# Token tiles' products: a float32 transpose by TensorE into the h banks and a split there, in place of a DMA transpose of the two split parts

## The chip, the cores and the metric

The kernel runs on one core of a Trainium2 chip, in one launch. The metric is the device time of that launch in microseconds; the median of three runs of the kernel before is 2922.66 us (2917.66 to 2924.61).

## What is computed

Three layers, one after the other, on 8 sequences of 3072 tokens with 256 channels: a filter in the frequency domain, a SoLU block with a layer norm, and a routed layer with eight experts.

```python
X = np.fft.rfft(x, axis=1)
y = np.fft.irfft(X * (filt_r + 1j * filt_i)[None], n=x.shape[1], axis=1)   # attn
x = y.reshape(B * S, D)
h = x @ w_in                                    # 256 -> 1024
e = np.exp(h - h.max(-1, keepdims=True))
sm = e / (e.sum(-1, keepdims=True) + 1e-09)
solu = h * sm
mu = solu.mean(-1, keepdims=True); var = ((solu - mu) ** 2).mean(-1, keepdims=True)
x = (((solu - mu) / np.sqrt(var + 1e-06)) * g_ln) @ w_out       # 1024 -> 256
xn = x / (np.linalg.norm(x, axis=-1, keepdims=True) + 1e-06)
logits = xn @ en.T / tau                        # en: unit expert embeddings
expert_idx = logits.argmax(1); probs = softmax(logits)
out[mask_e] = probs[.., e] * (np.maximum(x[mask_e] @ w1[e], 0) @ w2[e])
```

## The kernel before

The 24576 tokens go through as 192 tiles of 128 tokens, 48 for each of four pairs of sequences. Stage A is the FFT of a pair (`fft`, first stage at L487, second at L601 with the result z, the filter at L562 and L563, third at L635); the inverse's last stage is `inv4` (L672), which gives two tiles at once. Stage B (`stage_b`) takes the tiles one after the other through w_in and w_out and routes them. Stage C (`stage_c`) runs the experts over blocks of the tokens routed to them.

The order is the order of the code: `tc.manual_schedule()` leaves every engine's instructions as they are issued, and each engine works through its own list in order. Stage B is a loop over i with several tiles in flight:

- `begin(i + 1)` issues the 12 float32r matmuls of h (L688) into one of two PSUM tiles h of two banks each; `top(i + 1)` lets VectorE take the negative maximum nm (L828);
- for tile i ScalarE writes es = Exp(h + nm) (L840), VectorE multiplies h with es into es (L841, the "product"), ScalarE squares the product into h (L877), which gives the sum of squares for the factor cc (L886);
- for tile i - 1 ScalarE copies the product times cc to float16 (hl, L853), VectorE writes the rest to the other half of hl (L854), and SP transposes both, 128 x 2048 float16, by a DMA into T (L856);
- for tile j = i - LAG (LAG = 3) TensorE multiplies T with w_out in 24 float16 matmuls into o (L868); `half`, an iteration later, splits o into two float16 parts and SP stores them (rows, L894 to L899).

Beside the tiles of pair p the function `aux`, called twice per iteration, runs units of the FFT of pair p + 1: 24 units of its first stage, 8 with loads only, 64 of the second and third stage in groups of four (two z units, two third-stage units; the filter of the group before stands at the third). Beside the last pair it splits the experts' weights (`w_split`, L427 and L433). The FFT's loads and stores, the tiles' loads and stores and the transposes all go out on SP's queue. `early` makes the first tables of stage C beside the last tiles, one step per iteration.

Of the kernel before, what the change touches and what calls it, by code (L numbers as in the profile page):

```python
# [23 lines left out]
FF = 1024  # L24
# [9 lines left out]
LAG = 3  # L34
# [5 lines left out]
MAGIC = 0x5F3759DF  # L40

# [71 lines left out]
class Tags:  # L113
    """A pool with a number of buffers for each tag."""
# [16 lines left out]
class Tag:  # L131
    """One tag of a pool."""
# [6 lines left out]
class Turns:  # L139
    """A pool whose buffers are taken in turn."""  # L140
# [10 lines left out]
class Build:  # L151
# [72 lines left out]
    def scale(self, ps, sp, m, sc, isc):  # L224
        """[128, n] -> sc = 2^k with 4 <= max(m) * sc < 8, isc = 1 / sc, on all partitions."""
# [24 lines left out]
    def load_wide(self, out, src):  # L250
        """Loads 512 columns of float32, or of float64 (given as its bits), which it rounds to float32."""
# [25 lines left out]
    def prep_b(self, sp, ps):  # L277
        """MoE weights: w_in as two float32r parts; g * w_out, centred, with its product with the
        experts' embeddings, as two float16 parts."""
# [7 lines left out]
        def unit():  # L287
            """Unit embeddings, transposed."""
# [91 lines left out]
    def w_max(self, sp, ps):  # L380
        """Scales of the experts' weights: powers of two from their largest magnitudes."""
# [17 lines left out]
    def w_split(self, sp):  # L399
        """The experts' weights, resident, as two float16 parts."""  # L400
# [37 lines left out]
    def rsqrt(self, v, w, y, x, tmp, shape):  # L438
        """y = x^-1/2 by Newton's steps from the bit-level start; tmp: twice x's columns."""
# [10 lines left out]
    # ---------------------------------------------------------------- stage A  # L450
# [21 lines left out]
    def stage1(self, p, part, ap, ps, bufA):  # L472
        """The transform over n1, with the twiddle factors, of a part of the columns."""
# [19 lines left out]
    def catch_up(self):  # L493
        """Work that was put off until the engines have time for it."""
# [4 lines left out]
    def fft(self, p, ap, ps, hp):  # L499
        """Stages 1 to 3 for the pair of batches p, as a stream of units; the first pair in two parts  # L500
        of the columns, so that their stages overlap."""
# [18 lines left out]
        def first(j):  # L520
            """The unit's first k1, in the order 0 to 31, 63 to 32."""
            return j % NK // 2 * KC + j % 2 * (N1 // 2)
# [125 lines left out]
    def inv4(self, xp, ps):  # L648
        """Stage 4: yields, for two tiles at once, x transposed as float32r parts."""
# [29 lines left out]
    # ---------------------------------------------------------------- stage B  # L679
# [20 lines left out]
    def b_final(self, t, p, n2, gw, ps, snap):  # L700
        """Routing of a group's tokens: their factors and their places in the experts' lists."""
        nc = self.nc
        v, w = nc.vector, nc.gpsimd
        st, cc, raw = t["st"], t["cc"], t["raw"]
        Se, Ss, Sq = st[:, 0, :], st[:, 1, :], st[:, 2, :]
# [8 lines left out]
        # x = r * (row of products); V = (variance + 1e-6) * (sum of exponentials)^2  # L714
        rc = row("grc", 2)
        v.reciprocal(rc, cc)
        V = row("gV", 2)
        u = row("gu")
        w.tensor_scalar(V[:, 0, :], Se, 1e-9, None, op0=ALU.add)
        w.tensor_tensor(V[:, 0, :], V[:, 0, :], V[:, 0, :], op=ALU.mult)  # L720
# [19 lines left out]
        w.tensor_tensor(r, y[:, 0, :], rc[:, 0, :], op=ALU.mult)  # L740
        w.tensor_scalar(r, r, self.isc_o, None, op0=ALU.mult)
# [9 lines left out]
        w.tensor_tensor(r, r, rc[:, 1, :], op=ALU.mult)  # L751
# [51 lines left out]
    def stage_b(self, xp, bps, gp, ps, hp, op, aux, early):  # L803
        """aux(p, n2): runs the units that belong beside tile n2 of the pair p."""
# [19 lines left out]
        def top(i):  # L824
            L = live[i]
            L["pool"] = bps[0] if i < n - N2 else bps[1]
            L["nm"] = L["pool"].tile([128, 1], F32, name="nm", tag="nm")
            nc.vector.tensor_reduce(L["nm"], L["h"], axis=AX.X, op=ALU.max, negate=True)  # L828

        begin(0)  # L830
        top(0)
        for i in range(n + LAG):
            j = i - LAG
            now = 0 <= i < n
            if now:
                if i % G == 0:
                    groups[i // G] = self.b_group(gp)
# [3 lines left out]
                nc.vector.scalar_tensor_tensor(L["s"], L["h"], 1.0, L["s"], op0=ALU.mult, op1=ALU.mult, accum_out=col(i, "st", 1))  # L841
# [3 lines left out]
            if 0 <= i - 1 < n:  # L845
                M, cc = live[i - 1], col(i - 1, "cc", 0)
                P = M["pool"]
                if "hl" not in P.kept:
                    P.kept["hl"] = P.tile([128, 3 if P is bps[1] else 4, FF], F16, name="hl", tag="hl")
                r = 2 * ((i - 1) % 2)  # L850
                l = 1 if P is bps[1] else r + 1
                hl = P.kept["hl"]
                nc.scalar.activation(hl[:, r, :], M["s"], AF.Copy, scale=cc)  # L853
                nc.vector.scalar_tensor_tensor(hl[:, l, :], M["s"], cc, hl[:, r, :], op0=ALU.mult, op1=ALU.subtract)  # L854
                T = P.tile([128, 16, 128], F16, name="T", tag="T")
                nc.sync.dma_start_transpose(out=T, in_=hl[:, min(l, r):min(l, r) + 2, :].rearrange("p a b -> p (a b)"))  # L856
                M["T"] = (T, 8 if l < r else 0)
# [394 lines left out]
```

## Time and profile before

| | |
|---|---|
| median of three runs | 2922.66 us |
| profiled execution, span of its instructions | 2966.3 us |
| TensorE matmul / weight load | busy 2667.8 us (90%) / 2153.6 us (73%) |
| VectorE, ScalarE, GpSimd | busy 1920.5, 1447.2, 1445.9 us |
| stage A of the first pair alone | to about 215 us |
| stage B | about 215 to 1862 us |
| stage C | about 1862 us to the end |

The profile is one execution; for it only the span is known, and the timed runs are shorter than the span by 43.6 us, 1.5%. A busy TensorE is not one at its peak: a matmul's record has a length that overlaps with the next one's, so the pace is read from the distance between starts. Plain float32 matmuls are recorded as two.

### The profile page before, as it was taken

The page shows a single profiled execution, that of the slowest core. Times are in us where ns is not written, and L with a number is a line of the kernel's source. Part 1 is how long each engine was busy: PE and PEld are TensorE (multiplying, and loading weights), DVE is VectorE, ACT ScalarE, POOL GpSimd, SP SyncE. Part 2 cuts the span into 40 slices and gives each one's busy share as a digit, 9 for nine tenths or more (in the row PEclk, how much of TensorE's full clock was granted, in tenths as well). Part 3 has the DMA queues.
Part 4 walks back from the last instruction along what each step waited for, and adds up shares of the span by engine and source line. Part 5 has one row for each costly group of instructions (what it writes and reads, how often), then busy time and mean ns, then how long its engine had stood idle before and what let it go on. Part 6 is the DMA issues. An engine that isn't in the chain of part 4 may idle for free.

```text
span 2966.3 us, 52286 instructions
## 1 busy us (share of the span) xinstructions
PE 2667.8 (90%) x19262; PEld 2153.6 (73%) x19262; DVE 1920.5 (65%) x3013; ACT 1447.2 (49%) x2746; POOL 1445.9 (49%) x2237
## 2 busy tenths in 40 slices
PE   5788898989888988889998888899999999999997
PEld 4446666767666666656786677778888888888876
DVE  2755787856788855887878887445444444444454
ACT  3345666656556655556677776223333333333322
POOL 1420476623656523655647774654444444444432
PEclk8889998999889999989999999999999999999999
DMA  9869999899899999987878886222322222233222
GB/s 272 197 164 244 215 221 197 191 240 240 183 188 194 193 235 224 190 185 168 172 162 192 184 187 123 73 67 74 77 76 76 76 77 76 75 78 76 74 53 48
DMA packets 729551, 447.47 MB, mean 151 GB/s; under 512 B 535595, under 2 KB 656053, under 8 KB 726992
## 3 DMA queue, kind: packets, MB, share of 16 engines
q1 hardware_dynamic: 701920, 386.12, 60.4%
q0 software_dynamic: 27088, 57.48, 6.4%
q8 instruction: 152, 2.49, 0.4%
q14 instruction: 103, 0.84, 0.1%
q10 hardware_dynamic: 288, 0.55, 0.1%
HBM read 195.93 MB, written 103.35 MB: 101 GB/s over the span
## 4 chain that ended last, share of the span: by engine, by line
PE 32%; issue 22%; DMA 17%; POOL 16%; DVE 10%; ACT 2%; SPq 1%; POOLq 0%; another core or an unknown queue 0%; DVEq 0%; ACTq 0%
PE o L868 12%; DMA T<-hl 11%; PE h L688 9%; POOL crow L1039 6%; POOL out_dram L162 5%; POOL scr L161 3%; PE a L635 2%; PE a L487 2%; DVE hl L854 2%; PE a L672 2%; PE o L1106 1%; DMA mt<-in_m_dram 1%; DVE zw L562 1%; DVE nm L828 1%; PE a L601 1%
## 5 line engine op out<-in xcount | busy, mean ns | idle before, releaser
L868 PE MATMUL o<-wo_h,T 128*128 128x264 f16 x3072 | 602.2, 292 | 119.3 <-DMA T<-hl 67.4
L868 PEld LDWEIGHTS <-T 128*128 128x128 f16 x4608 | 469.0, 104 | 244.3 <-DMA T<-hl 82.8
L1106 PE MATMUL o<-cw,chh 128*128 128x256 f16 x3184 | 534.8, 274 | 10.3 <-ACT chh L1097 9.3
L1094 PEld LDWEIGHTS <-cw 128*128 128x128 f16 x5280 | 477.7, 98 | 60.1 <-issue 9.2
L162 POOL DMA_INDIRECT out_dram<-cot,ids x199 | 206.0, 1035 | 503.8 <-ACT cot L1109 492.2
L868 PE MATMUL o<-wo_l,T 128*128 128x264 f16 x1536 | 449.3, 293 | 0.0
L1106 PE MATMUL o<-cw,chl 128*128 128x256 f16 x1592 | 435.9, 274 | 10.9 <-DVE chl L1098 10.2
L1098 DVE SCALAR_TENSOR_TENSOR chl<-h,chh 128x512 f16<-128x512 f32 x199 | 136.1, 684 | 410.3 <-ACT chh L1097 392.4
L1106 PEld LDWEIGHTS <-chh 128*128 128x128 f16 x3184 | 309.9, 98 | 51.8 <-ACT chh L1097 16.0
L841 DVE SCALAR_TENSOR_TENSOR es<-h,es 128x1024 f32<-128x1024 f32 x192 | 234.9, 1223 | 171.5 <-ACT es L840 162.1
L688 PE MATMUL h<-win_h,xh 128*128 128x512 f32 x768 | 319.4, 416 | 1.3 <-ACT xh L675 0.7
L840 ACT ACTIVATE es<-h,nm 128x1024 f32<-128x1024 f32 x192 | 214.1, 1115 | 206.8 <-DVE gcc L886 194.8
L688 PE MATMUL h<-win_h,xl 128*128 128x512 f32 x768 | 302.4, 394 | 0.0
L1094 PE MATMUL a<-cxT,cw 128*128 128x256 f16 (+1 forms) x2640 | 296.4, 264 | 5.0 <-issue 5.0
L688 PE MATMUL h<-win_l,xh 128*128 128x512 f32 x768 | 300.3, 391 | 0.0
L1094 PE MATMUL h<-cxT,cw 128*128 128x256 f16 (+1 forms) x2640 | 295.4, 263 | 3.9 <-DVE cw L1067 3.9
L1109 ACT ACTIVATE cot<-o,fac 128x256 f32<-128x256 f32 x199 | 94.5, 475 | 419.0 <-PE o L1106 416.8
L1067 DVE COPY cw<-wexp 128x4096 f16 x220 | 279.6, 1279 | 22.3 <-issue 6.0
L854 DVE SCALAR_TENSOR_TENSOR hl<-es,gcc,hl 128x1024 f16<-128x1024 f32 x192 | 262.9, 1369 | 27.0 <-DMA T<-hl 18.1
L828 DVE TENSOR_REDUCE nm<-h 128x1 f32<-128x1024 f32 x192 | 233.5, 1216 | 65.4 <-PE h L688 64.8
L162 POOL DMA_INDIRECT lst<-gdi,gix x192 | 244.6, 1274 | 38.0 <-issue 26.8
L1039 POOL DMA_INDIRECT crow<-xs,ids x199 | 198.3, 997 | 72.2 <-issue 66.0
(239 smaller groups left out, 4594.0 us busy)
## 6 DMA issues: line engine op xcount, KB each, us to landing
wst<-in_w_dram SPq DMA_DIRECT2D x128, 256.0 KB
in<-in_x_dram SPq DMA_DIRECT2D x48, 512.0 KB
bufA<-out SPq DMA_DIRECT2D x96, 256.0 KB
in<-bufA SPq DMA_DIRECT2D x64, 384.0 KB
bufC<-out SPq DMA_DIRECT2D x128, 192.0 KB
c<-bufC SPq DMA_DIRECT2D x96, 256.0 KB
xs<-rows SPq DMA_DIRECT2D x96, 256.0 KB
ft<-in_filt_dram SPq DMA_DIRECT2D x24, 960.0 KB
```

The source lines that it names most:

```text
L162: ins = self.nc.gpsimd.indirect_dma_start(in_offset=None, **kw).ins
L688: nc.tensor.matmul(h[:, nb, :], l[:, i, db, :], r[:, db, sl], start=k == 0, stop=k == 5)
L828: nc.vector.tensor_reduce(L["nm"], L["h"], axis=AX.X, op=ALU.max, negate=True)
L840: nc.scalar.activation(L["s"], L["h"], AF.Exp, bias=L["nm"], accum_out=col(i, "st", 0))
L841: nc.vector.scalar_tensor_tensor(L["s"], L["h"], 1.0, L["s"], op0=ALU.mult, op1=ALU.mult, accum_out=col(i, "st", 1))
L854: nc.vector.scalar_tensor_tensor(hl[:, l, :], M["s"], cc, hl[:, r, :], op0=ALU.mult, op1=ALU.subtract)
L868: nc.tensor.matmul(o[:, :D + E], T[:, l, :], r[:, f, :], start=q == 0, stop=q == 23)
L1039: nc.gpsimd.indirect_dma_start(out=rows[:, h, :], out_offset=None, in_=self.xs, in_offset=bass.IndirectOffsetOnAxis(ap=tab["ids"][:, h, k: ...
L1067: nc.vector.tensor_copy(w.rearrange("p (o k) -> p o k", o=1), self.wexp[:, bass.ds(e, 1), part * 4096:(part + 1) * 4096])
L1094: nc.tensor.matmul(t[:, i, :], w1[:, l, db, f * 128:(f + 1) * 128], xT[:, r + db, :n], start=q == 0, stop=q == 5)
L1098: nc.vector.scalar_tensor_tensor(hl[:, sl, :n], t, 0.0, hh[:, sl, :n], op0=ALU.max, op1=ALU.subtract)
L1106: nc.tensor.matmul(o[:, :D], l[:, f, h * 128:(h + 1) * 128], w2[:, r, f, :], start=q == 0, stop=q == 23)
```

## The change

Per tile, `turn(i)` issues eight float32 transposes of the product es by TensorE into the tile's own h, whose values are no longer needed, 128 columns each. ScalarE then copies h times 16384 to the first half of T in float16, and VectorE writes the rest to the second half. hl and the DMA transpose are gone. So that h is not written by the square any more, the square goes to a bfloat16 buffer jk. The factor cc must be known before the product: it comes from nm with two column operations in `top`, and the product is taken with it; `b_final` follows suit. LAG is 2, `aux`'s first call stands ahead of `begin`, `early` starts two iterations later, and some start-up buffers have other names. The compiled program has 1536 more matmuls and as many more weight loads, eight of each for a tile.

```diff
-LAG = 3
+LAG = 2
+SS = 16384.0
...
-        rc = row("grc", 2)
-        v.reciprocal(rc, cc)
+        rc = row("grc")
+        v.reciprocal(rc, cc[:, 1, :])
...
         w.tensor_scalar(V[:, 0, :], Se, 1e-9, None, op0=ALU.add)
+        w.tensor_tensor(V[:, 0, :], V[:, 0, :], c1, op=ALU.mult)
...
-        w.tensor_tensor(r, y[:, 0, :], rc[:, 0, :], op=ALU.mult)
-        w.tensor_scalar(r, r, self.isc_o, None, op0=ALU.mult)
+        w.tensor_scalar(r, y[:, 0, :], self.isc_o, 1.0 / SS, op0=ALU.mult, op1=ALU.mult)
...
         def top(i):
+            if i % G == 0:
+                groups[i // G] = self.b_group(gp)
...
             nc.vector.tensor_reduce(L["nm"], L["h"], axis=AX.X, op=ALU.max, negate=True)
+            cc = col(i, "cc", 0)
+            nc.vector.tensor_scalar(cc, L["nm"], L["nm"], 1.0, op0=ALU.mult, op1=ALU.max)
+            nc.vector.tensor_scalar(cc.bitcast(I32), cc.bitcast(I32), -0.5, float(MAGIC), op0=ALU.mult, op1=ALU.add)
+
+        def turn(i):
+            M = live[i]
+            h = M["h"]
+            for f in range(8):
+                nc.tensor.transpose(h[:, f * 128:(f + 1) * 128], M["s"][:, f * 128:(f + 1) * 128], self.ident)
+            T = M["T"] = M["pool"].tile([128, 16, 128], F16, name="T", tag="T")
+            hi, lo = (T[:, k:k + 8, :].rearrange("p a b -> p (a b)") for k in (0, 8))
+            nc.scalar.activation(hi, h, AF.Copy, scale=SS)
+            nc.vector.scalar_tensor_tensor(lo, h, SS, hi, op0=ALU.mult, op1=ALU.subtract)
...
+            if 0 <= i - 1 < n:
+                turn(i - 1)
             if now:
...
-                nc.vector.scalar_tensor_tensor(L["s"], L["h"], 1.0, L["s"], op0=ALU.mult, op1=ALU.mult, accum_out=col(i, "st", 1))
+                nc.vector.scalar_tensor_tensor(L["s"], L["h"], col(i, "cc", 0), L["s"], op0=ALU.mult, op1=ALU.mult, accum_out=col(i, "st", 1))
...
-                nc.scalar.activation(hl[:, r, :], M["s"], AF.Copy, scale=cc)
-                nc.vector.scalar_tensor_tensor(hl[:, l, :], M["s"], cc, hl[:, r, :], op0=ALU.mult, op1=ALU.subtract)
-                T = P.tile([128, 16, 128], F16, name="T", tag="T")
-                nc.sync.dma_start_transpose(out=T, in_=hl[:, min(l, r):min(l, r) + 2, :].rearrange("p a b -> p (a b)"))
...
             if now:
+                aux(*divmod(i, N2), 0)
                 if i + 1 < n:
                     begin(i + 1)
-                aux(*divmod(i, N2), 0)
-                if i + 1 < n:
                     top(i + 1)
-                sq = col(i, "st", 2)
-                nc.scalar.activation(L["h"], L["s"], AF.Square, accum_out=sq)
+                jk = L["pool"].tile([128, FF], BF16, name="jk", tag="jk")
+                nc.scalar.activation(jk, L["s"], AF.Square, accum_out=col(i, "st", 2))
...
-                cc = col(i, "cc", 0)
-                nc.vector.tensor_scalar(cc.bitcast(I32), sq.bitcast(I32), -0.5, float(MAGIC + (14 << 23)), op0=ALU.mult, op1=ALU.add)
...
-            if i >= n - N2 + SPLIT:
+            if i >= n - N2 + SPLIT + 2:
                 next(early, 0)
```

Three places show how the engines' lists change. Line numbers of the kernel after are higher by a few.

VectorE before, in an iteration with the filter (zw, y); es is the product, hl the rest of the split, nm the maximum of the next tile:

```order
L841 SCALAR_TENSOR_TENSOR es,gst<-h,es 128x1024
L854 SCALAR_TENSOR_TENSOR hl<-es,gcc,hl 128x1024
L895 SCALAR_TENSOR_TENSOR rows<-o,gcc,rows 128x256
L562 SCALAR_TENSOR_TENSOR zw<-zw,cst,ft 96x1024
L563 TENSOR_TENSOR y<-y,zw 96x1024
L393 TENSOR_REDUCE wm_a<-wst 128x1
L828 TENSOR_REDUCE nm<-h 128x1
L886 TENSOR_SCALAR gcc<-gst 128x1
L889 COPY graw<-o 128x8
L890 TENSOR_SCALAR gcc<-gn_7528 128x1
```

VectorE after, in such an iteration and the first operation of the next; T written from h is the rest of the split:

```order
L847 SCALAR_TENSOR_TENSOR T<-h,T 128x1024
L860 SCALAR_TENSOR_TENSOR es,gst<-h,gcc,es 128x1024
L898 SCALAR_TENSOR_TENSOR rows<-o,gcc,rows 128x256
L563 SCALAR_TENSOR_TENSOR zw<-zw,cst,ft 96x1024
L564 TENSOR_TENSOR y<-y,zw 96x1024
L833 TENSOR_REDUCE nm<-h 128x1
L835 TENSOR_SCALAR gcc<-nm 128x1
L836 TENSOR_SCALAR gcc<-gcc 128x1
L892 COPY graw<-o 128x8
L893 TENSOR_SCALAR gcc<-gn_8186 128x1
L718 RECIPROCAL grc<-gcc 128x8
L847 SCALAR_TENSOR_TENSOR T<-h,T 128x1024
```

The rest of the split has moved from behind the product to the head of the iteration, ahead of it, and reads h.

TensorE before, from the end of h to the o of the next iteration, beside the FFT's third stage:

```order
L688 MATMUL h<-win_h,xh 128x512
L688 MATMUL h<-win_l,xh 128x512
L688 MATMUL h<-win_h,xl 128x512
L635 MATMUL a<-y,cst_95 96x512 x2
L672 MATMUL a<-mt_11363,c_11361 128x128 x4
L868 LDWEIGHTS T
L868 MATMUL o<-wo_h,T 128x264
```

TensorE after, the same stretch:

```order
L689 MATMUL h<-win_h,xh 128x512
L689 MATMUL h<-win_l,xh 128x512
L689 MATMUL h<-win_h,xl 128x512
L636 MATMUL a<-y,cst_95 96x512
L843 MATMUL h<-cst,es 128x128 x8
L673 MATMUL a<-mt_12442,c_12440 128x128 x4
L874 LDWEIGHTS T
L874 MATMUL o<-wo_h,T 128x264
```

The eight transposes stand between an iteration's last FFT unit and stage 4 or o; one of the two FFT units has gone ahead of h.

SP before, in the FFT's first stage (bufA is its result, wst a piece of the experts' weights, c and mt stage 4's input):

```order
L856 DMA_TRANSPOSE T<-hl 128x16x128
L899 DMA xs<-rows 128x512
L491 DMA bufA<-out 64x4x256 x2
L389 DMA wst<-in_w_dram 128x512
L659 DMA c_10284<-bufC 128x512
L661 DMA mt_10286<-in_m_dram 128x256
L856 DMA_TRANSPOSE T<-hl 128x16x128
```

SP after, at the end of that stage:

```order
L902 DMA xs<-rows 128x512
L492 DMA bufA<-out 64x4x256 x2
L531 DMA ft<-in_filt_dram 96x2560
L390 DMA wst<-in_w_dram 128x512
L537 DMA in<-bufA 96x1024 x2
L660 DMA c_11432<-bufC 128x512
```

Nothing stands between the loads and stores any more.

## Rows read from the trace of the kernel before

**Rows 1.** Busy time of each engine by stretch; then granted clock, DMA share, GB/s.

```profile
215.00:1512.00 1297.00, 1144.61 (x6602) 868.85 (x6602) 973.31 (x1601) 791.31 (x1540) 635.01 (x1075) 0.94 0.95 203
1512.00:1862.00 350.00, 303.74 (x2036) 248.20 (x2034) 286.56 (x596) 244.98 (x485) 225.51 (x440) 0.97 0.77 170
```

**Rows 2.** Waits of TensorE, 215 to 1512 us: total, times, longest.

```profile
PE o L868 <- DMA T<-hl: 67.4, 40, 5.8
PE a L601 <- DVE xl L676: 27.2, 16, 2.7
```

**Rows 3.** The stretches again, h matmuls (L688) alone: length, busy (xcount), then loads.

```profile
595.00:697.00 102.00, 32.94 (x132) 23.97 (x132) 0.97 1.07 244
697.00:736.00 39.00, 15.00 (x60) 10.90 (x60) 0.96 1.09 228
736.00:1006.00 270.00, 84.50 (x336) 61.26 (x336) 0.91 0.93 189
...
1512.00:1600.00 88.00, 39.04 (x156) 28.33 (x156) 1.00 0.78 177
1600.00:1841.00 241.00, 102.01 (x408) 74.09 (x408) 0.98 0.77 172
```

**Rows 4.** TensorE in order of time, two tiles: start us, length us, instruction.

```profile
514.45 0.27 PE L868 MATMUL o<-wo_h,T 128*128 128x264 f16 x1
...
517.06 0.48 PE L688 MATMUL h<-win_h,xh 128*128 128x512 f32 x1
...
519.90 0.40 PE L601 MATMUL a<-hi,d2h 96*96 96x512 f32 x1
...
521.46 1.16 PE L672 MATMUL a<-mt,c 128*128 128x128 f32 x8
522.45 0.28 PE L868 MATMUL o<-wo_h,T 128*128 128x264 f16 x1
...
527.92 1.88 PE L635 MATMUL a<-y,cst 96*96 96x512 f32 x4
529.63 0.28 PE L868 MATMUL o<-wo_h,T 128*128 128x264 f16 x1
```

**Rows 5.** SP's DMA transposes in the view of line L856: ns min/median/max.

```profile
L856 SPq DMA_TRANSPOSE T<-hl x192: 1317/3585/8397, 223.1 to 1854.5; - x192
```

**Rows 6.** Costliest groups of the page: busy us, mean ns | idle before.

```profile
L841 DVE SCALAR_TENSOR_TENSOR es<-h,es 128x1024 f32<-128x1024 f32 x192 | 234.9, 1223 | 171.5 <-ACT es L840 162.1
L840 ACT ACTIVATE es<-h,nm 128x1024 f32<-128x1024 f32 x192 | 214.1, 1115 | 206.8 <-DVE gcc L886 194.8
...
L854 DVE SCALAR_TENSOR_TENSOR hl<-es,gcc,hl 128x1024 f16<-128x1024 f32 x192 | 262.9, 1369 | 27.0 <-DMA T<-hl 18.1
```

**Rows 7.** TensorE's weight loads in order of time, at 63 and at 521 us.

```profile
63.05 0.97 PEld L330 LDWEIGHTS o<-penT,pwT 128*128 128x128 f32 x8
...
521.45 0.97 PEld L672 LDWEIGHTS a<-mt,c 128*128 128x128 f32 x8 [0.45 <-ACT z L602]
```

**Rows 8.** VectorE and TensorE in order of time around one filter.

```profile
1288.95 0.48 DVE L895 SCALAR_TENSOR_TENSOR rows<-o,gcc,rows 128x256 f16<-128x256 f32 x1
...
1289.35 3.09 DVE L562 SCALAR_TENSOR_TENSOR zw<-zw,cst,ft 96x1024 f32<-96x1024 f32 x1
...
1292.54 3.20 DVE L563 TENSOR_TENSOR y<-y,zw 96x1024 f32<-96x1024 f32 x1
...
1295.66 1.21 DVE L828 TENSOR_REDUCE nm<-h 128x1 f32<-128x1024 f32 x1
...
1300.10 0.48 PE L601 MATMUL a<-hi,d2h 96*96 96x512 f32 x1 [2.11 <-DVE xl L676]
```

**Rows 9.** The filter's first product in the view of its line: ns min/median/max.

```profile
L562 DVE SCALAR_TENSOR_TENSOR zw<-zw,cst,ft x48: 1265/3016/3205, 348.7 to 1465.8; 96x1024 f32<-96x1024 f32 x45, 96x768 f32<-96x768 f32 x3
```

**Rows 10.** TensorE in order of time: last h matmul, first expert matmul.

```profile
1838.93 0.39 PE L688 MATMUL h<-win_h,xl 128*128 128x512 f32 x1
...
1865.97 1.44 PE L1094 MATMUL h<-cxT,cw 128*128 128x256 f16 x6 [3.93 <-DVE cw L1067]
```

More of the change, by code (lines that the diff above doesn't have):

```diff
@@ L704, in b_final @@
         st, cc, raw = t["st"], t["cc"], t["raw"]
+        c1 = cc[:, 0, :]
         Se, Ss, Sq = st[:, 0, :], st[:, 1, :], st[:, 2, :]
@@ L750, in b_final @@
         w.tensor_tensor(d, raw, bc(rn), op=ALU.mult)
-        w.tensor_tensor(r, r, rc[:, 1, :], op=ALU.mult)
+        w.tensor_tensor(r, r, rc, op=ALU.mult)
         yield
@@ L834, in stage_b @@
             now = 0 <= i < n
+            if 0 <= i - 1 < n:
+                turn(i - 1)
             if now:
-                if i % G == 0:
-                    groups[i // G] = self.b_group(gp)
                 L = live[i]
@@ L844, in stage_b @@
                 xs.append(next(src, None))
[L845 to L852, printed above, removed]
-                nc.scalar.activation(hl[:, r, :], M["s"], AF.Copy, scale=cc)
-                nc.vector.scalar_tensor_tensor(hl[:, l, :], M["s"], cc, hl[:, r, :], op0=ALU.mult, op1=ALU.subtract)
-                T = P.tile([128, 16, 128], F16, name="T", tag="T")
-                nc.sync.dma_start_transpose(out=T, in_=hl[:, min(l, r):min(l, r) + 2, :].rearrange("p a b -> p (a b)"))
-                M["T"] = (T, 8 if l < r else 0)
             if half:
@@ L862, in stage_b @@
             if 0 <= j < n:
-                T, k = live.pop(j)["T"]
+                T = live.pop(j)["T"]
                 o = op.tile([128, 512], F32, name="o", tag="o")
@@ L866, in stage_b @@
                 for f in range(8):
-                    for l, r in ((k + f, self.wo_h), (k + f, self.wo_l), (8 - k + f, self.wo_h)):
+                    for l, r in ((f, self.wo_h), (f, self.wo_l), (8 + f, self.wo_h)):
                         nc.tensor.matmul(o[:, :D + E], T[:, l, :], r[:, f, :], start=q == 0, stop=q == 23)
@@ L973, in table @@
             in_offset=bass.IndirectOffsetOnAxis(ap=ri[:K].bitcast(U32), axis=0)).ins
+        assert len(self.scattered["lst"]) >= (self.np_run * N2 // G - (3 if start is None else 0)) * G
         for name in self.scattered["lst"]:
@@ L1134, in run @@
             bps = [None, None]
-            bps[0] = right.enter_context(Tags(tc, "bx", {"nm": 2, "es": 2, "hl": 1, "T": 3}, side="right"))
+            bps[0] = right.enter_context(Tags(tc, "bx", {"nm": 2, "es": 2, "jk": 1, "T": 3}, side="right"))
             ap = right.enter_context(tc.tile_pool(name="ap", bufs=2, side="right"))
@@ L1144, in run @@
                     prep = self.prep_b(pp, Tag(op, "o"))
-                    spare = bps[0].tile([128, 16, 128], F32, name="hl", tag="hl")
-                    self.m1 = [spare[:, 4 * k:4 * k + 4, :] for k in range(4)]
+                    spare = pp.tile([128, 12, 128], F32, name="m1s")
+                    self.m1 = [spare[:, 4 * k:4 * k + 4, :] for k in range(3)]
+                    self.m1.append(bps[0].tile([128, 4, 128], F32, name="jk", tag="jk"))
                     for pool, tag in ((xp, "c4"), (xp, "xh"), (xp, "xl"), (gp, "rows")):
@@ L1166, in last_pool @@
                     mid.close()
-                    bps[1] = mid.enter_context(Tags(tc, "bp", {"nm": 2, "es": 2, "hl": 1, "T": 2}))
+                    bps[1] = mid.enter_context(Tags(tc, "bp", {"nm": 2, "es": 2, "jk": 1, "T": 2}))
                 if last == 0:
```

## Prediction

> **What bounds the kernel now.** I read the stretches first, then the waits, then the order of one tile pair in time. From 215 to 1512 us (the tiles of the first three pairs of batches, beside which the FFT of the next pair runs) the 16 DMA engines are taken to 0.95 of the time, TensorE is busy for 1144.6 of 1297 us, and its granted clock is 0.94, that is, it spends about an eighth of the stretch at 1.2 GHz and the rest at 2.4 GHz [rows 1]. TensorE's largest wait there is that of the o matmuls for the transposed parts T, 67.4 us in 40 places; the next is 27.2 us in front of FFT matmuls, put down to VectorE [rows 2]. Three engines are therefore near their limits at once: DMA, TensorE and, in places, VectorE. The last pair (1512 us on) has no FFT, and DMA is at 0.77.
>
> The three pairs are not alike inside. Twelve h matmuls make one tile, so the counts give the tiles [rows 3]: in the second pair 11 tiles with the FFT's first stage take 102 us, 5 tiles with nothing but loads 39 us (7.8 each), 28 tiles with its second and third stage 270 us (9.64 each). The last pair takes 6.77 us a tile at first, then 7.09 with the splitting of the experts' weights.
>
> What TensorE needs at full clock is read off two tiles in a row [rows 4]: o 2.61 us, h 2.84, two second-stage units 1.56, stage 4 for two tiles 0.99, o and h of the next tile 5.47, two third-stage units 1.71. Together 15.18, or 7.59 us a tile; without the FFT units 11.91, or 5.96.
>
> **What the change removes.** 192 DMA transposes of 512 KB. SP is held 3.6 us (median) by each [rows 5], in front of the FFT's loads and stores on the same queue; both come earlier now. The 67.4 us of waits for T go. What is late next has to be found by stage, below. ScalarE's copy and VectorE's rest (1.37 us on average) of the split are not removed, they only change their source from SBUF to PSUM. The nearest rows are VectorE's product of h with es, 1.22 us with one operand in PSUM, and ScalarE's Exp from PSUM, 1.11 us [rows 6]; I take 1.25 and 1.15 and book neither gain nor loss. ScalarE's square of the product goes to a buffer in SBUF and no longer into h; of the column operations on VectorE there are two in place of one. Both are counted as nothing: they stand behind the large operations of engines that wait for TensorE in most tiles, and where VectorE does not wait they are in the handovers below.
>
> **What it adds on TensorE.** Eight float32 transposes per tile, one weight load and one matmul each, the loads in float32. The trace has no transpose, but it has float32 loads of 128 columns in a row: eight take 0.97 us ahead of 128-column matmuls, and eight take the same 0.97 us ahead of matmuls of 8 columns [rows 7]. So the load sets the pace there, 0.97 / 8 = 0.12 us each. Bounds: not much less than 0.9 us a tile, since even an 8-column matmul does not go faster; not more than 0.24 each, if a transpose, like the plain float32 matmul of stage 4 (eight records for four matmuls [rows 4]), goes through twice. I take 0.95 us for the eight, as the load is what both rows have in common with a transpose. 192 x 0.95 = 182 us of new TensorE work, which the waits and slow clock of today must pay for. The tile floor becomes 8.54 us with FFT units, 6.91 without, say 6.95 with the turn from one kind of matmul to another.
>
> The Trainium skill ("TensorE: Matmul & The Clock Gate", Part 4: PE-mode transpose) speaks against this: it gives about 275 ns for one 128x128 transpose in a kernel's context. Eight would be 2.2 us by that page, an estimate that would add 240 us to my sum. It looks like the length of one instruction with its latency, as an o matmul here lasts 0.27 us while 24 of them take 2.61, 0.11 each [rows 4]; but no run here shows a transpose, so it stays as a rival.
>
> **The new waits.** h has two buffers. Until now h(i+1) waited for ScalarE's square into the old h; now it waits until VectorE has read the transposed product out of that buffer (lo). The order shows lo as the first VectorE operation of an iteration, so it stands behind all that the iteration before has queued: the filter's two products zw and y, the maximum nm and the column operations. Who waits for it: h, and behind it an FFT unit and the next transposes on TensorE. The first FFT unit of an iteration now stands ahead of h, not behind it, which delays h by up to 0.86 us where h does not wait anyway; it is in the sums of the floor. LAG 2 for 3 only shortens the end of the stage, below.
>
> *Tiles without the filter.* Transposes end, hi 1.15, lo 1.25: about 2.6 us with handovers, while TensorE does o (2.61) and half the time stage 4. h does not wait. Transposes of the next tile need Exp (1.1) and the product (1.22) after hi: 3.7 us, by when TensorE is in h. So these tiles run at TensorE's floor. First-stage tiles: 11 x 6.95 + 24 units x 0.86 (as many columns as a third-stage unit) = 97 us for 102: -5, three times -15. Load-only tiles: 5 x 6.95 = 35 for 39: -4, three times -12. Some 12 tiles per run without any FFT, and 13 of the last pair: 25 x (6.95 - 6.77) = +4. The last 34, where VectorE scales the experts' weights too, I put at 7.2 for 7.09: +4.
>
> *Tiles with the filter* come once in two tiles of the long phase. There zw takes 3.09 and y 3.20 us, next to GpSimd's products; zw's minimum is 1.27 us and its median of 48 is 3.02 [rows 8, 9], so more than half are slow; I take two in three. nm starts only after them, at 1295.7, and at 1300.1 TensorE has idled for 2.1 us [rows 8]. After the change: lo 1.25, product 1.22, rows 0.48, zw and y 6.29, nm 1.21, lo 1.25 = 11.7 us of VectorE in a row; only then h 2.84, the second of two FFT units 0.78, transposes 0.95, hi 1.15 = 5.7; with column operations, weight maxima and handovers, 1.6 us by my estimate, 19.0 us for two tiles. Today it is 19.3 (270 / 14). With a fast filter VectorE is not late and TensorE's 15.18 + 1.9 = 17.1 holds. Two to one: 18.4, or -0.44 a tile; 28 tiles three times: -37 us. That is the cover gone: what DMA gave back, the h buffer mostly takes.
>
> *The end of the stage.* The last h matmul ends at 1839.3, the first expert matmul starts at 1866.0 [rows 10]: 26.7 us. Now: transposes, hi, Exp, product, transposes, hi, lo, o and 3.93 us to the first expert matmul, 0.95 + 1.15 + 1.1 + 1.2 + 0.95 + 1.15 + 1.25 + 2.6 + 3.9 = 14.3, with handovers and some slow clock 17.5: -9. The first slot's rows are gathered two tiles later than before; they have about 14 us, so I count nothing, and 3 us more if they are late.
>
> *Reserve.* At clock 0.94 about 156 us of the 1297 are at half clock, which costs up to 78 us. My floors are at full clock, and I leave a quarter of it, 20 us, and 12 us of waits for the FFT's loads, which still come over the same queue: +32.
>
> Sum: -15 - 12 - 37 + 4 + 4 - 9 + 32 = -33 us. The sum is made against the profiled execution, whose span is 2966.3 us; the median of the timed runs is 2922.7, 1.5% less. Scaled by that the sum hardly changes, so **2890 us**.
>
> **Rivals.**
> *A transpose costs more than its load* (slower). Place: the head of every iteration on TensorE. If load and matmul do not overlap, each costs 0.055 us more (half an o matmul's 0.11), +0.44 us a tile, 192 tiles: +84, 2974 us; with two passes +0.12 each, about 3070. From 33 / 1536 = 0.02 us more than 0.12, so 0.14 us each, the gain is gone. For it: no transpose in the trace. Against it: loads and matmuls overlap in all float32 rows. 0.19.
> *Transposes follow each other at a record's full length*, 0.27 us as an o matmul's: 8 x 0.27 - 0.95 = +1.2 us a tile, +232, 3122 us. 0.04. The figure of the Trainium skill's page above is nearly that length.
> *VectorE binds the long phase fully*: every filter at the slow price and no gain there: +37, 2927 us. For it: zw and y meet GpSimd's products at the same point of the order as before. 0.22, of which a third ends above 2931.
> *The filter gets out of GpSimd's way*, as the tile's rhythm shifts: 28 slow periods (two thirds of 42) come down by 1.9: -53, 2837 us. 0.10.
>
> **How the numbers follow.** Forecast 2890 with 0.45. Its own range is 2862 to 2915. A measurement of this kernel tells about 0.3% (8.8 us) from no change, so below 2914 counts as faster: 0.45 + 0.10 less 0.02 for the forecast's edge = 0.53; same 0.15 of VectorE's case and that edge = 0.17; slower 0.07 + 0.19 + 0.04 = 0.30. The range for 8 in 10 is 2835 to 2980: it leaves out a transpose at two passes or at a record's full length, and a little of the last rival.
>
> **What would show it.** Right: transposes 0.12 us apart; no wait of o for T; h waiting for lo in every second tile of the long phase, near 2 us, and hardly elsewhere; DMA well under 0.95 before 1512 us and granted clock above 0.96; first expert matmul some 17 us after the last h. Wrong: transposes 0.17 us or more apart; waits in front of the transposes for the product es; tiles of the last pair above 7.4 us; a clock that stays at 0.94.

## Result and profile after

The kernel after takes 2892.6 us (median of four runs, 2891.1 to 2893.5) against 2922.7 for the kernel before: a ratio of 0.9902, interval 0.9888 to 0.9916, or 30 us less. The prediction was 2890, 33 less. Its profiled execution spans 2891.7 us. The two spans, 2966.3 and 2891.7, must not be subtracted: in the first one stage C, whose code the change leaves alone, takes 35 us longer (first experiment).

The stretches of the profile after, as in [rows 1] (us; busy time of TensorE, its loads, VectorE, ScalarE, GpSimd; granted clock, DMA share, GB/s):

```profile
215.00:1512.00 1297.00, 1241.64 (x7997) 1012.23 (x7996) 992.12 (x1804) 819.09 (x1582) 600.60 (x1122) 0.99 0.56 147
1512.00:1862.00 350.00, 339.46 (x2471) 288.75 (x2470) 273.96 (x613) 230.29 (x464) 209.15 (x447) 0.99 0.35 95
```

From 215 to 1512 us (in the kernel after, the first three pairs and the first 30 us of the last) DMA fell from 0.95 to 0.56 of the time, TensorE's busy time rose from 1144.6 to 1241.6 us, so that it now idles for 55 us and not for 152, and its granted clock rose from 0.94 to 0.99: it stays at 2.4 GHz nearly throughout. TensorE now sets the time of the tiles (e1 and e10 below). Its waits there, as in [rows 2]:

```profile
PE h L689 <- DVE T L847: 24.6, 24, 2.0
PE a L602 <- DVE gpos L784: 22.7, 7, 4.1
```

The wait of o for T is gone. In its place h waits for lo (L847, VectorE's rest of the split, the last reader of the old h), as forecast, and z units (L602) wait for gpos, which nobody had on the list: `b_final` counts a group's tokens with matmuls into one of the two PSUM tiles "a" that the FFT units use too, and VectorE frees it (L784) only behind lo and the product of the next tile.

The transposes, in the view of their line and as one tile's eight in time, followed by o (start us, length us):

```profile
L843 PEld LDWEIGHTS h<-cst,es x1536: 137/141/147, 216.5 to 1815.4; 128*128 128x128 f32 x192
L843 PE MATMUL h<-cst,es x1536: 270/273/331, 216.7 to 1815.5; 128*128 128x128 f32 x192
```

```profile
836.62 1.04 PE L843 MATMUL h<-cst,es 128*128 128x128 f32 x8
837.49 0.28 PE L874 MATMUL o<-wo_h,T 128*128 128x264 f16 x1
```

One record is 0.27 us long, but eight and the way to o take 0.87 us: (1.04 - 0.27) / 7 = 0.11 us from start to start. One float32 transpose is one load and one matmul record.

The second pair, h matmuls alone, as in [rows 3] (first stage of the FFT; loads only; second and third stage):

```profile
594.40:692.20 97.80, 37.32 (x144) 27.00 (x144) 1.00 0.70 198
692.20:724.70 32.50, 12.06 (x48) 8.71 (x48) 1.00 0.63 170
724.70:986.80 262.10, 94.02 (x348) 68.19 (x348) 0.97 0.58 138
```

That is 12, 4 and 29 tiles, 45 in 392 us, for 44 in 411 before. The end of the stage, answering [rows 10]:

```profile
1808.70 0.39 PE L689 MATMUL h<-win_h,xl 128*128 128x512 f32 x1
...
1826.49 1.87 PE L1098 MATMUL h<-cxT,cw 128*128 128x256 f16 x8 [3.94 <-DVE cw L1071]
```

From the end of the last h matmul to the first expert matmul it is 17.4 us, for 26.7.

### The profile page after: what moved, and what is told of

Its sections match the earlier page's. It is cut to its first block, busy times and chain, and to the rows that moved or that the text cites. A ratio compares the mean times of both kernels' runs of the same rounds, so it can differ in the third digit from the quotient of the medians.

```text
span 2891.7 us, 54694 instructions
## 1 busy us (share of the span) xinstructions
PE 2749.9 (95%) x20798; PEld 2306.4 (80%) x20798; DVE 1906.8 (66%) x3205; ACT 1450.4 (50%) x2746; POOL 1368.0 (47%) x2237
## 4 chain that ended last, share of the span: by engine, by line
PE 43%; issue 21%; POOL 16%; DVE 14%; DMA 3%; ACT 1%; POOLq 0%; SPq 0%; DVEq 0%; ACTq 0%
PE h L689 16%; PE o L874 11%; POOL crow L1043 6%; POOL out_dram L163 6%; PE h L843 4%; POOL scr L162 3%; PE a L488 3%; DVE y L564 3%; DVE zw L563 2%; PE a L673 2%; DVE T L847 2%; PE a L636 2%; DVE nm L833 2%; PE a L602 2%; DVE es L860 1%
## 5 line engine op out<-in xcount | busy, mean ns | idle before, releaser
L874 PE MATMUL o<-wo_h,T 128*128 128x264 f16 x3072 | 551.1, 276 | 1.2 <-DVE gcc L893 1.2
L1110 PE MATMUL o<-cw,chh 128*128 128x256 f16 x3184 | 528.9, 273 | 0.0
L874 PEld LDWEIGHTS <-T 128*128 128x128 f16 x4608 | 451.7, 98 | 66.3 <-ACT rows L888 1.5
L874 PE MATMUL o<-wo_l,T 128*128 128x264 f16 x1536 | 424.6, 276 | 0.0
L689 PE MATMUL h<-win_h,xh 128*128 128x512 f32 x768 | 337.4, 439 | 30.2 <-DVE T L847 29.0
L847 DVE SCALAR_TENSOR_TENSOR T<-h,T 128x1024 f16<-128x1024 f32 x192 | 233.4, 1216 | 67.7 <-ACT T L846 65.4
L846 ACT ACTIVATE T<-h 128x1024 f16<-128x1024 f32 x192 | 196.4, 1023 | 125.0 <-PE h L843 123.0
L860 DVE SCALAR_TENSOR_TENSOR es<-h,gcc,es 128x1024 f32<-128x1024 f32 x192 | 244.6, 1274 | 0.8 <-ACT es L859 0.8
L163 POOL DMA_INDIRECT lst<-gdi,gix x192 | 226.7, 1181 | 36.7 <-issue 27.6
```

The lines of the kernel that those rows point to most:

```text
L689: nc.tensor.matmul(h[:, nb, :], l[:, i, db, :], r[:, db, sl], start=k == 0, stop=k == 5)
L846: nc.scalar.activation(hi, h, AF.Copy, scale=SS)
L847: nc.vector.scalar_tensor_tensor(lo, h, SS, hi, op0=ALU.mult, op1=ALU.subtract)
L860: nc.vector.scalar_tensor_tensor(L["s"], L["h"], col(i, "cc", 0), L["s"], op0=ALU.mult, op1=ALU.mult, accum_out=col(i, "st", 1))
L874: nc.tensor.matmul(o[:, :D + E], T[:, l, :], r[:, f, :], start=q == 0, stop=q == 23)
L1110: nc.tensor.matmul(o[:, :D], l[:, f, h * 128:(h + 1) * 128], w2[:, r, f, :], start=q == 0, stop=q == 23)
```

## Experiments

The runs were on several chips, and the median of the kernel before differs between these: 2932 us beside the first four runs, 2917 beside the next four, 2970 and 2961 beside the last ones. So the table has, beside ratios, the length of stage B (start of the first to end of the last h matmul) from each profile, the part that the edits touch. Where two runs are compared, their stage B is.

Each stage B is that of one execution. For e0, e4 and e9 that execution is at the fast end of its own timed runs: 2924 us for a median of 2935, 2867 for 2877, 2945 for 2951. Where it matters, the medians stand beside it.

| kernel | median, us | ratio to before, same chip | stage B, us |
|---|---|---|---|
| before (first profile) | 2922.7 | | 1630.2 |
| e0: before again | 2935.4 | 1.001 [0.999, 1.003] | 1622.3 |
| after | 2892.6 | 0.990 [0.989, 0.992] | 1601.1 |
| e1: after, transposes twice | 3021.2 | 1.029 [1.027, 1.032] | 1723.3 |
| e2: before without DMA transposes | 2795.4 | 0.953 [0.951, 0.955] | 1499.0 |
| e3: after with DMA transposes | 2959.9 | 1.010 [1.006, 1.014] | 1663.0 |
| e4: count read at once | 2877.1 | 0.987 [0.984, 0.990] | 1575.9 |
| e5: GpSimd out of the filter | 2851.7 | 0.976 [0.974, 0.979] | 1556.7 |
| e6: e4 and e5 | 2839.3 | 0.973 [0.971, 0.975] | 1544.6 |
| e7: FFT unit behind h | 2968.1 | 1.017 [1.014, 1.020] | 1675.4 |
| e8: after with LAG 3 | 2916.6 | 0.981 [0.977, 0.986] | 1591.1 |
| e9: before, FFT unit ahead of h | 2951.3 | 0.994 [0.992, 0.996] | 1614.3 |
| e10: e6, transposes twice | 3005.5 | 1.012 [1.007, 1.016] | 1684.4 |
| e11: half of e5 | 2878.9 | 0.972 [0.967, 0.976] | 1555.1 |

**What the span of before was worth (e0).** No edit.

> The kernel before, unchanged, profiled once more. The span on which the prediction's sum was made, 2966.3 us, is 43.6 above the timed median. Theory: that one execution was disturbed, above all in stage C (first expert matmul to the end 1100 us, against 1065 in the kernel after, whose code there is the same). Then this profile spans about 2921 us, stage C takes about 1065, and the first to the last h matmul of stage B takes some 1620 to 1630. Rival: stage C really is 35 us longer in the kernel before; then it shows 1100 again and stage B must be the shorter one, near 1590.

The span, and in order of time the first expert matmul:

```profile
core 0: 2922.4 us, clock 0.957
```

```profile
1856.65 2.72 PE L1094 MATMUL h<-cxT,cw 128*128 128x256 f16 x12 [3.96 <-DVE cw L1067]
```

Stage C takes 2922.4 - 1856.6 = 1065.8 us, where [rows 10] and the first span give 1100.3, and 1065.2 in the kernel after. It was not a disturbance: in e8 to e11, on the chips where the kernel before takes 2961 to 2970 us, stage C is 1094 to 1097 us again, with the same code, and in all others 1065 to 1068. So it goes with the chip; why is not settled, and on which chip the first profile was taken is not known. From before again to after, stage B is 21.2 us shorter and the stretch behind it 8.3 (25.7 to 17.4), with 1.2 from the other stages 30.7 in all. That this is so near the timed 30 owes something to luck: e0's profiled execution, 2924 us, lies near the 2922.7 of the first chip and not near its own median of 2935.

**What a transpose costs (e1, e10).**

```
-            for f in range(8):
+            for f in (*range(8), *range(8)):
                 nc.tensor.transpose(h[:, f * 128:(f + 1) * 128], ...
```

> The kernel after with each of the eight transposes of a tile issued twice in a row into the same place (16 per tile, 1536 more in all); nothing else changes. Theory (TensorE sets the time of the tiles now, a transpose costs its distance of 0.109 us): 1536 x 0.109 = 167 us more, and no idle time takes any of it up since hi, lo and the next h stand behind the transposes: 3045 to 3070 us. Rival (transposes lie in time in which TensorE would wait anyway): less than +60, below 2955. Second rival (a transpose costs more than its distance shows, through clock or memory): over +200, above 3090.

> The kernel with both edits (routing count at once, GpSimd out of the filter's way), with every transpose issued twice as in e1. Theory: that kernel has only 16 us of idle TensorE in the first three pairs and next to no half clock left to absorb, so the 1536 x 0.109 = 167 us of added work show nearly in full: +145 to +167, 2985 to 3006 us. Rival (part of a second transpose is hidden whatever waits there are): +129 as in e1 or less, below 2970.

Stage B grows by 122 us in e1, less than 167 and far more than 60: between the theory and its rival. The waits give part of the difference:

```profile
PE a L602 <- DVE gpos L784: 16.6, 7, 3.3
PE h L689 <- DVE T L847: 12.2, 17, 1.5
```

TensorE idles 21 us less (its busy time in the first three pairs allows 34 us of idling, for 55), which fits VectorE's having a longer tile to do its work in, and it is at half clock for 7 us of stage B in place of 37, worth 15. 167 - 21 - 15 = 131, near the 122. In e10, where 16 us of idling were left, stage B grows by 140 us, 5 under what was expected; its median lies in the expected range only because stage C takes 27 us more on that chip than for e6. TensorE idles 4 us there, so that 12 us are filled up and some 15 of the 167 are unexplained. In time a second transpose costs 0.08 us (e1, 122 / 1536) and 0.09 (e10); with the idle time and the half clock that it fills up added back, both give 0.10. So TensorE bounds the stage.

**What the DMA transposes cost (e2, e3).** In e2 only the first two tiles of each pool are transposed by DMA in the kernel before; in e3 they come back into the kernel after, into a buffer that nobody reads:

```
+                Ts = P.kept.setdefault("Ts", [])
+                if len(Ts) < 2:
+                    T = P.tile([128, 16, 128], F16, name="T", tag="T")
+                    nc.sync.dma_start_transpose(out=T, in_=hl[:, min(l, r):min(l, r) + 2, :].rearrange("p a b -> p (a b)"))
+                    Ts.append(T)
+                T = Ts[(i - 1) % 2]
```

```
+            U = M["pool"].tile([128, 16, 128], F16, name="U", tag="U")
+            nc.sync.dma_start_transpose(out=U, in_=T.rearrange("p a b -> p (a b)"))
```

> The kernel before, but only the first two tiles of each buffer pool are transposed by DMA; all later tiles' o matmuls read those two T again (so the products of the other tiles are left out of the result; every other instruction stays). What the removal alone is worth. Theory: waits of o for T (67), the other waits of TensorE that come from late loads, and the half clock (170 us of the first four pairs, worth half of that) all go, up to 165 us, with the VectorE part of the filter periods left: 2757 to 2830 us, granted clock of the long stretch above 0.98. Rival A: only the 67 us of waits for T go: about 2855. Rival B: another wait (the filter on VectorE) takes their place: above 2882.

> The kernel after, with a DMA transpose of T into a buffer U that nothing reads, once per tile, on SP's queue behind lo (T has two buffers for three in the first three pairs). Nobody waits for U's content; only traffic, SP's hold and the use of T's buffers come back. Theory (traffic and the held queue cost time of their own: FFT loads come late, TensorE idles and falls to half clock): 2920 to 2980 us, DMA share above 0.9 and granted clock below 0.97 in the first three pairs. Rival (only the wait of o for T cost time): 2883 to 2902, no difference that can be told.

The removal alone is worth 123 us of stage B, nearly twice the 67 us of waits for T, and 137 us by the medians on that chip (2932 and 2795); the time lies in the theory's range. It may hold more than the transposes, as in e2 o waits for no split of its own tile either. The expected clock of 0.98 was not reached; the first of the following rows (stretch from 215 to 1512 us) is of e2, the second of e3:

```profile
215.00:1512.00 1297.00, 1216.71 (x7339) 944.36 (x7337) 1071.14 (x1811) 880.20 (x1718) 728.58 (x1221) 0.97 0.60 157
```

```profile
215.00:1512.00 1297.00, 1204.07 (x7572) 971.95 (x7571) 947.53 (x1706) 781.32 (x1507) 575.40 (x1058) 0.97 0.92 200
```

Brought back where nobody waits for their result, they cost 62 us. TensorE's waits in e3:

```profile
PE h L689 <- DVE T L847: 30.9, 26, 2.6
PE a L602 <- DVE gpos L784: 20.4, 6, 4.2
PE a L673 <- DMA mt<-in_m_dram: 14.0, 6, 5.5
PE a L488 <- DMA mt<-in_m_dram: 7.8, 6, 2.2
```

22 us are waits for loads (mt) on SP's queue, where the transposes stand too, and the clock falls from 0.99 to 0.97. Part of the 62 is the experiment's own: ScalarE's hi waits 25.7 us in 13 places until the DMA has read T, which has one buffer fewer here:

```profile
ACT T L846 <- DMA U<-T: 25.7, 13, 5.1
```

So traffic and queue cost time by themselves, but their size is only bounded by 62.

From e2 to after, stage B grows by 102 us: by the 167 us of transposes and the new waits, less the idle time and half clock that they fill up. The shares weren't taken apart.

**The unforeseen wait and the filter (e4, e5, e6, e11).** e4 takes one `yield` out of `b_final`, so that gpos is issued directly behind the matmuls it reads, ahead of the next lo. e5 moves two operations of GpSimd: its product (L624) straight behind the last z unit, the split of the next input (L546) from the head of the iteration to behind its first FFT unit. e6 is both. e11 moves the product alone.

```
-        yield 2
         rg = row("grg")
```

In e5 `hand` holds the loads of zw and GpSimd's product, which stood further below; e11 has only this first part:

```
+                    if p > 0 and i > 0:
+                        zs[j] = hand(j, z)
                     next(other, 0)
                     yield
...
-            self.catch_up()
...
                 aux(*divmod(i, N2), 0)
+                self.catch_up()
```

> The kernel after, with the routing step that reads a group's running count out of PSUM (gpos, L784) issued directly behind the matmuls that make it, in the same iteration, and so ahead of the next lo on VectorE, not behind the next product. Theory: the PSUM buffer comes free before TensorE needs it, the seven waits of z units for gpos in the first three pairs (22.7 us, 4.1 at most) and the half clock that follows some of them (34 us at half clock in all) go: 2855 to 2875 us, h's waits for lo (24.6) stay. Rival (another wait takes the place, for the same units wait for VectorE anyway): 2885 to 2895.

> The kernel after, with GpSimd's two large operations of a filter group moved ahead of the filter in the program: the product y of z with the real part straight behind the last z unit, and the split of the next input (hi on ScalarE, its rest on GpSimd) behind the iteration's first FFT unit rather than at the iteration's head. The work is the same. Theory (VectorE's zw and y wait while GpSimd works on its product, and that decides the long phase): the filter takes 2.5 us in nearly all of 45 cases, for 6.3 in 20 of them; each slow period loses 1.3 to 2 us and h's waits for lo go: 2845 to 2870 us. Rival (the filter's length is covered and TensorE's floor and the routing waits decide): 2885 to 2895 although zw and y are short.

> Both edits together: the routing count read at once, and GpSimd's operations out of the filter's way. Theory (two causes that add): TensorE idles less than 15 us in 215 to 1512 us (55 in the kernel after) and the two-tile period is 16.7 us nearly everywhere: 2830 to 2855 us. Rival (they overlap, either alone gives all): no more than 5 us below the better of the two.

> The kernel after with only half of the GpSimd edit: its product y stands straight behind the last z unit, its part of the input's split stays at the head of the filter's iteration. In the kernel after a slow zw (3.2 us) ends 1.08 us after GpSimd's split does and a slow y (3.3 us) 1.08 us after GpSimd's product does. Theory (each of VectorE's two operations waits for the GpSimd operation beside it): y takes 1.22 us nearly everywhere, zw still 2.5 to 3.2 in about 20 of 45, the slow filter is 4.4 us for 6.4, and about half of the whole edit's 41 us is had: ratio to before 0.980 to 0.986. Rival (a large GpSimd operation slows whatever VectorE does beside it, in proportion): zw and y both near 2.2 us, sum unchanged.

A slow filter of the kernel after, GpSimd and VectorE in order of time (start us, length us):

```profile
841.19 2.40 POOL L546 TENSOR_TENSOR in<-in,hi 96x1024 fp32r<-96x1024 f32 x1 [7.65 <-ACT hi L544]
...
841.49 3.19 DVE L563 SCALAR_TENSOR_TENSOR zw<-zw,cst,ft 96x1024 f32<-96x1024 f32 x1
...
843.56 3.33 POOL L624 TENSOR_TENSOR y<-z,ft 96x1024 f32<-96x1024 f32 x1
...
844.71 3.27 DVE L564 TENSOR_TENSOR y<-y,zw 96x1024 f32<-96x1024 f32 x1
```

zw starts 0.3 us after GpSimd's split and ends at 844.68, 1.09 us after the split's end at 843.59; y ends at 847.98, 1.09 us after GpSimd's product at 846.89. Neither uses a result of the GpSimd operation beside it: each is held until that one's end and then runs. (zw and y alone take 1.28 and 1.22.) GpSimd's product, which meets zw, takes 3.33 us itself, and 2.36 in e11's line below. The view of the filter's lines, in ns min/median/max, the first of the kernel after, the second of e5, the third of e11:

```profile
L563 DVE SCALAR_TENSOR_TENSOR zw<-zw,cst,ft x48: 1008/1444/3193, 341.1 to 1427.1; 96x1024 f32<-96x1024 f32 x45, 96x768 f32<-96x768 f32 x3
```

```profile
L563 DVE SCALAR_TENSOR_TENSOR zw<-zw,cst,ft x48: 1003/1272/3011, 343.6 to 1384.2; 96x1024 f32<-96x1024 f32 x45, 96x768 f32<-96x768 f32 x3
```

```profile
L563 DVE SCALAR_TENSOR_TENSOR zw<-zw,cst,ft x48: 1004/1272/3102, 343.8 to 1383.2; 96x1024 f32<-96x1024 f32 x45, 96x768 f32<-96x768 f32 x3
L564 DVE TENSOR_TENSOR y<-y,zw x48: 1220/1221/3446, 347.0 to 1384.5; 96x1024 f32<-96x1024 f32 x48
```

In e5 no filter is above 4.5 us, where 21 of 48 were near 6.4, and stage B is 44 us shorter. Half the edit (e11) gives all of it, in stage B as in the ratio (0.972, for 0.980 to 0.986 expected): y was freed as expected, all but four, and zw nearly everywhere too, which was not. Once the periods are shorter, the split no longer falls beside zw in most of them. Which of several shifts does that was not looked into. Where zw still meets GpSimd in e11, it again ends 1.08 us after it:

```profile
528.88 2.36 POOL L575 TENSOR_TENSOR y<-z,ft 96x1024 f32<-96x1024 f32 x1
...
529.32 3.00 DVE L563 SCALAR_TENSOR_TENSOR zw<-zw,cst,ft 96x1024 f32<-96x1024 f32 x1
```

That VectorE waits in full, and does not run in proportion slower, falls out of e11 against its rival. The Trainium skill ("SBUF — State Buffer", Who interferes with whom) says it as a rule: a VectorE operation with two inputs in SBUF and a GpSimd operation that reads SBUF exclude each other, and the later one blocks until the first is done. The trace agrees: in the kernel after all 43 slow zw and y of 96x1024 end 1.08 or 1.09 us after a large GpSimd operation does. It also agrees with the Trainium skill's sentence there that one input in SBUF, outside the two-port modes, doesn't contend: lo and the product, with h in PSUM, take 1.22 and 1.27 us beside GpSimd as without it.

e4 is 25 us of stage B in its profiled execution, but that is the fastest of four between 2867 and 2889: by the median it is 15 us, by the ratios to before 10, and the median misses the expected upper end by 2. The waits for gpos fall from 22.7 to 5.7 us, those of h for lo rise to 31.9, where they were to stay at 24.6:

```profile
PE h L689 <- DVE T L846: 31.9, 33, 2.0
PE a L602 <- DVE gpos L783: 5.7, 7, 1.7
```

Together (e6) the two give 56 us of stage B, 12 more than e5 alone (12 by the medians too, on one chip), and TensorE's waits of 215 to 1512 us are nearly gone:

```profile
PE h L696 <- DVE T L853: 15.6, 26, 1.8
PE a L643 <- DVE gpos L790: 0.4, 1, 0.4
```

e6 is faster than both kernels, by 2.7% [2.5, 2.9] against before.

**The place of the FFT unit, and LAG (e7, e9, e8).** e7 undoes one part of the change, e9 does it alone in the kernel before. The edit of e9 (e7 is its reverse):

```
+                aux(*divmod(i, N2), 0)
                 if i + 1 < n:
                     begin(i + 1)
-                aux(*divmod(i, N2), 0)
-                if i + 1 < n:
                     top(i + 1)
```

> The kernel after, with the iteration's first FFT unit issued behind the next tile's h again, as in the kernel before. Theory: the unit (0.86 us) no longer covers the wait of h for lo, so h's waits for lo grow from 25 to some 45 us; the z units' waits for gpos (23 us) shrink to nearly nothing because h's 2.84 us stand ahead of them: the two cancel, 2885 to 2910 us. Rival (the place of the unit is of no account): both rows unchanged. Second rival (the edit is what makes the kernel after fast): above 2920.

> The kernel before with this one part of the change alone: the iteration's first FFT unit ahead of the next tile's h. Theory (the unit's place matters only where h waits for VectorE's lo, which the kernel before doesn't have): within 12 us of before. Rival (the place of the unit is worth its 75 us in either kernel): 30 us or more below before.

> The kernel after with LAG 3 as in the kernel before (and with a third T buffer beside the last pair, which that distance needs, and the early tables one step later). Theory: the distance itself is worth one o of 2.6 us at the end of the stage and nothing in the tiles, so most of the 8.3 us between last h and first expert matmul came from the DMA transpose that is gone: 2893 to 2902 us, that stretch 20 to 21 us for 17.4. Rival (the distance makes the tiles faster too): above 2910.

The largest miss of these runs: e7 was expected near the kernel after, and its stage B is 74 us longer. Its largest wait of TensorE, 215 to 1512 us:

```profile
PE h L689 <- DVE T L847: 88.0, 82, 4.2
```

As expected the waits for gpos went and those of h for lo grew, but to 88 us and not 45, in 82 places and not 24. Of the 82, 54 are shorter than the unit's 0.86 us: ahead of h it hides such waits whole, in far more tiles than the 24 in which a rest of the wait was left to see. Of the 74 us some 55 are accounted for, by TensorE's idle time in stage B (106 us for 60) and half clock (55 us for 37); the rest wasn't traced. The second rival holds: with the unit behind h, the kernel after would be slower than before, at 1.017. In the kernel before the same edit gives 0.6% [0.4, 0.8], some 17 us, 5 more than the theory allowed and far from 75: its place is worth much only where h waits for lo.

LAG 3 makes the stretch behind the last h 21.3 us (17.4), as expected, but stage B 10 us shorter, on another chip and with another T buffer; the waits for gpos are gone from its larger ones, and those of h for lo are 42.5 us. Its 2916.6 us are in the range of the rival, though not for the rival's reason: stage C takes 1097 us there, and stage B isn't longer. That the distance is worth nothing but the end isn't shown.

## Why the prediction was right

The forecast was met within 3 us. To see whether for its reasons, the profile of before again is set against that of after by kinds of tiles: the distance between one tile's Exp and the next's, sorted by the FFT matmuls that start in it. Both have 34 tiles with first-stage units, 92 with second- or third-stage units, 18 with none in the first three pairs, 47 in the last pair. It is one execution of each, so a term is good to a few us.

| term | predicted | measured |
|---|---|---|
| tiles with the first stage | -15 | 300.1 to 288.4: -12 |
| tiles without FFT, first three pairs | -12 | 131.0 to 125.1: -6 |
| long phase, with the reserve | -37 + 32 = -5 | 861.6 to 854.6: -7 |
| no FFT any more, last pair | +4 + 4 | 324.5 to 330.3: +6 |
| end of the stage | -9 | 25.7 to 17.4: -8 |
| sum | -33 | -27, timed -30 |

**The price of a transpose: right.** 0.12 us each was taken from float32 loads in [rows 7]; the distance is 0.109, 15 us less in all than the 182 booked. Rivals with load and matmul apart (0.175) or a record's full length fall with it. The figure of 275 ns on the page of the Trainium skill ("TensorE: Matmul & The Clock Gate", Part 4: PE-mode transpose) is nearly the record's length here, 273 ns, and not the pace. The granted clock is 0.99 with eight per tile and 1.00 in e1 with sixteen, so no loss of clock shows beside them.

**hi and lo, booked at nothing: right.** hi takes 1.02 us and lo 1.22, for the 1.15 and 1.25 taken; the product went from 1.22 to 1.27. The lines of the page that answer [rows 6]:

```profile
L847 DVE SCALAR_TENSOR_TENSOR T<-h,T 128x1024 f16<-128x1024 f32 x192 | 233.4, 1216 | 67.7 <-ACT T L846 65.4
L846 ACT ACTIVATE T<-h 128x1024 f16<-128x1024 f32 x192 | 196.4, 1023 | 125.0 <-PE h L843 123.0
L860 DVE SCALAR_TENSOR_TENSOR es<-h,gcc,es 128x1024 f32<-128x1024 f32 x192 | 244.6, 1274 | 0.8 <-ACT es L859 0.8
```

**Tiles without the filter and the end: right.** 6.95 us was the floor put on tiles without FFT; 125.1 / 18 is 6.95, and the last pair has 7.03. The gain in the first three pairs is half of that booked, because these tiles took 7.28 us before (131.0 / 18) and not the 7.8 of [rows 3]. The end was put at 17.5 and is 17.4; e8 says that of the 8.3 us about 4 are LAG's.

**The long phase: right in sum, by two errors that cancel, which is luck.** Two tiles with a fast filter were put at 17.1 us; in the second and third pairs 12 of 16 such periods are 16.6 to 16.7. With a slow one 19.0 was expected; where nothing else waits it is 18.0 to 19.1, with h waiting 1 to 1.7 us for lo, not quite the 2 forecast. Slow are 21 of 48 and not two in three (28 of 48 in the kernel before). All this errs on the dear side. In place of it came the waits for gpos, 22.7 us in the first three pairs, which also bring two-tile periods of 20 to 23 us. The step that missed them is the one that lists who waits for the new h: it followed h, the FFT unit and the transposes, but not the PSUM tiles "a" that routing and FFT share. Nor was the half clock forecast in its place (37 us of stage B, half of that lost). The reserve of 32 us paid for both, so its size was right and its reason, late loads and half clock, only half so: no load is among the larger waits any more.

**The FFT unit ahead of h: the step that failed.** It was booked as a delay of up to 0.86 us within the floor. e7 shows that it is what keeps the tiles at their floor: 74 us of stage B hang on it, 62 of them in the tiles of the long phase and 13 in those of the first stage. That h does not wait in first-stage tiles was true only because of it: in e7 it waits in 16 of them, in the kernel after in one. Tiles without FFT units have nothing to put ahead of h, and e7 leaves them as they are. The forecast was right there because its floor was reached, for a reason that it didn't see.

**The last rival, GpSimd out of the way (2837 us), is no longer a guess:** it didn't happen by itself, but made by hand it gives 2852 (e5), and with the count read at once 2839 (e6).

## What to carry over

Work that moves from a queue to a busy engine pays for itself only from that engine's idle time and lost clock: here 123 us came back and 102 went into the new work and its waits, and the small rest depended on the order in which independent work stands ahead of the new wait. When a buffer gets a new last reader, look at what can be issued ahead of its next writer, and follow every pool that the waiting engine shares, not only the one that changed. Where VectorE and GpSimd both have operations with all inputs in SBUF, place them so that they don't meet.

## What the runs showed of the hardware

- VectorE's zw and y, with their inputs in SBUF, stop for GpSimd's large operations: 3.2 us for 1.28, ending 1.08 us after GpSimd's. Its lo and product, with one input in PSUM, don't.
- A float32 transpose of 128x128 is one load of 0.14 us and one matmul record of 0.27 us, and they follow each other every 0.109 us. Doubling their number cost 0.08 to 0.09 us each (e1, e10).
- Transposes by DMA whose result nobody waits for cost up to 62 us through the queue and the buffers that they hold.
- The same stage C takes 1065 to 1068 us on some chips and 1094 to 1100 on others. TensorE's waits in it, first of e0 and then of e8, name VectorE and ScalarE, whose chl and chh come late there, and they cover some half of the 30 us; what lies behind was not looked into:

```profile
PE o L1106 <- DVE chl L1098: 5.0, 4, 3.0
```

```profile
PE o L1110 <- DVE chl L1102: 11.6, 25, 2.2
PE o L1110 <- ACT chh L1101: 8.8, 21, 1.0
```
